# Turning q and k by 64 tokens on the two halves of TensorE's rows, and one PV and one weight turn for both tail steps, in a thresholded attention followed by a leaky-ReLU MLP

## The chip, the cores and the metric

The kernel runs on one core of a Trainium2 chip. Its time is the device time of one execution in microseconds (us); lower is better. The core has five engines that run side by side, each through its own list of instructions in order: TensorE (PE; its weight loads are shown as PEld), VectorE (DVE), ScalarE (ACT), GpSimd (POOL) and SyncE (SP), which issues most DMAs. TensorE writes to PSUM, eight banks per partition; GpSimd cannot read those, so VectorE and ScalarE empty them.

## What is computed

Eight batches of eight heads, 576 tokens, head dimension 64, in float32. Scores within `tau` of their row's maximum are kept, the others are dropped; the softmax of what is kept weighs `v`. The heads of a token are then joined to 512 features and go through a two-layer MLP with 2048 hidden features.

```python
    scale = 1.0 / np.sqrt(q.shape[-1])
    scores = scale * np.matmul(q, k.transpose(0, 1, 3, 2))
    thresh = np.max(scores, axis=-1, keepdims=True) - tau
    scores = np.where(scores >= thresh, scores, -1000000000.0)
    scores = scores - np.max(scores, axis=-1, keepdims=True)
    attn = np.exp(scores)
    attn = attn / (np.sum(attn, axis=-1, keepdims=True) + 1e-09)
    return np.matmul(attn, v).astype(np.float32)
...
    h = x @ w_in
    g = np.maximum(0.01 * h, h)
    return (g @ w_out).astype(np.float32)
```

## The kernel before

**Steps.** The work is a list of 144 steps, 18 per batch (`PERB`). A main step handles 128 query tokens of one pair of heads against all 576 keys: a batch has 2 blocks of 256 tokens x 4 pairs (`p`) x 2 halves (`c`), 16 steps. The last 64 tokens of a batch (512 to 575) are the tail: steps 16 and 17 of each batch take them, two pairs of heads at once. A loop over `n` (L487) writes out, for each `n`, instructions of several steps at different ages; every engine runs its instructions in just this order.

**q and k.** They arrive as float32 in `raw` tiles (`load_main`, 4 buffers) and `rawt` tiles for the tail (`load_tails`, 2 buffers). A unit is one pair of heads of q or of k, or the tail of q or k for all pairs: ten units per batch. GpSimd scales a unit by 64 and splits it into a high and a low fp16 half (`split_scale`, `split_high`, `split_low`, tile `half`). TensorE then turns it so that the head dimension lies on the partitions (`turn`, L162 to L188): 16 transposes for a main unit, 8 for a tail unit. Each has 64 columns of `half` over all 128 partitions as its weights and the 128 x 128 identity as the moving operand, and the two heads of a pair go to the upper and lower 64 output partitions, that is to the two halves of TensorE's columns. The result stands in one PSUM tile `tp` of the tag "h" and one VectorE copy moves a main unit, 128 x 1024 numbers, into `qT` or `kT`; a tail unit takes two copies of 128 x 256. L400 to L405 set when: the ten units of batch `b` from the third on are turned in steps 4, 5, 7, 9, 11, 13, 14, 16, 18 and 20 counted from the start of the batch before (`base`), with the GpSimd work three and two steps earlier. The units of batches 0 and 1 have times of their own.

**One pass of the loop.** Loads that are due (SP); `exps` of step n-1 (three ScalarE passes); `scores` of step n: 12 matmuls with 64 rows each, the two heads on the two halves of TensorE's rows, into the four PSUM banks of the tag "sc"; `copy_min` (VectorE: two passes out of PSUM that also give the row maxima); GpSimd's split work and `threshold` (GpSimd from step 28 on, VectorE before); `weights` of step n-1 (VectorE). Every second step, after a pair's second half, follow `recip` (VectorE), `widen` (GpSimd, writes the reciprocal beside the weights) and `turn_w`, a transposing DMA from SP that turns the weights `w` into `wT`. Then comes one unit of the first MLP layer (`layer1`, PSUM tile `hp` of the tag "h", emptied by ScalarE), the turns that are due, up to two pieces of the second layer (`layer2`, tag "o"), and `pv` with `evacuate`: the weighted sum of `v` for the step that is `PV_LAG` = 4 steps old, into the PSUM tag "pv", emptied by VectorE with a multiplication by the reciprocal.

**PSUM.** "sc" has four banks (one step's scores), "h" two, "pv" one and "o" one: all eight are taken.

**Tails.** Each tail step has its own pair tile, `recip`, `widen`, `turn_w` (128 x 1280), `pv` (20 matmuls of 64 columns) and `evacuate` (128 x 128). Tails of two batches make one group of 128 tokens for the MLP.

**The end.** After step 143 the loop runs on with what is left: the last PVs, `layer1` and `layer2` of the last groups, and the stores.

Of the kernel before, what the change touches and what calls it, by code (L numbers as in the profile page):

```python
# [10 lines left out]
FP16 = mybir.dt.float16  # L11
# [3 lines left out]
PV_LAG = 4  # L15
# [23 lines left out]
def kernel(  # L39
# [122 lines left out]
    def turn(key, copy=None):  # L162
# [24 lines left out]
        else:  # L187
            copy(out=dst[:, :, p, ds(c0, 512)], in_=tp[:, :, :, :].rearrange("d x t p -> d x (t p)"))  # L188

    steps = []
# [27 lines left out]
    def copy_min(st):  # L220

        st.mn = sb.tile([128, 2, 2], FP32, tag="mn", bufs=3, name="mn")
        st.s = sb.tile([128, 2, 576], FP32, tag="s", bufs=2, name="s")
        for h in range(2):
            nc.vector.tensor_scalar(  # L225
                out=st.s[:, h, :].rearrange("p (a b) -> p a b", a=2), in0=st.sc[h][:, :, 0:288],
                scalar1=-1.0 / UNIT, scalar2=None, op0=AX.mult, op1=AX.min, accum_out=st.mn[:, h, 0:1])

    def threshold(st):
        st.th = sb.tile([128, 2, 2], FP32, tag="th", bufs=3, name="th")  # L230
        eng = nc.vector if st.n < 28 else nc.gpsimd
        eng.tensor_scalar(out=st.th[:, :, 0], in0=st.mn[:, :, 0], scalar1=1.0, scalar2=tau_f, op0=AX.mult, op1=AX.add)  # L232

    def exps(st):

        c = 0 if st.tail else st.c
        if c == 0:
            pairs["now"] = pr = Pair()
            pr.w = sb.tile([128, 2, 10, 128], FP16, tag="w", bufs=3, name="w")
            pr.sum = sb.tile([128, 2, 2], FP32, tag="sum", bufs=3, name="sum")  # L240
            pr.n = 1 if st.tail else 2
        st.pair = pr = pairs["now"]
        flat = pr.w[:, c, :, :].rearrange("q n d -> q (n d)")
        st.w = [flat[:, ds(576 * h, 576)] for h in range(2)]
        st.sum = [pr.sum[:, c, h : h + 1] for h in range(2)]
        st.e = sb.tile([128, 576], FP16, tag="e", bufs=2, name="e")
        for h in range(2):
            if h:
                z = st.s[:, h, :]
                nc.scalar.activation(out=z, in_=z, func=AF.Prelu, bias=st.th[:, h, 0:1], scale=-1.0, alpha=1e20)  # L250
                nc.scalar.activation(out=st.w[h], in_=z, func=AF.Exp, bias=minus_tau[:, :], scale=1.0,  # L251
                                     accum_out=st.sum[h])
# [25 lines left out]
    def turn_w(pr):  # L278
        new_wt(pr)
        nc.sync.dma_start_transpose(out=pr.wt[:, 0 : pr.n, :, :].rearrange("k c n q -> k (c n) q"),  # L280
                                    in_=pr.w[:, 0 : pr.n, :, :].rearrange("q c n d -> q (c n d)"))
# [12 lines left out]
    def pv(st):  # L294
        st.pv = ps.tile([128, 4, 128], FP32, tag="pv", bufs=1, name="pv")
        wt = st.pair.wt
        for u in range(2 if st.tail else 1):
            for i in range(5):
                for h in range(2):
                    blk = i if h == 0 else 9 - i  # L300
                    rhs = wt[:, 0, blk - (blk > 4), ds(64 * u, 64)] if st.tail else wt[:, :, blk - (blk > 4), :]
                    o = st.pv[ds(64 * h, 64), 0, ds(64 * u, 64)] if st.tail else st.pv[ds(64 * h, 64), 0:2, :]
                    nc.tensor.matmul(out=o, lhsT=v16[st.b % 2][:, st.p + u, blk, :], rhs=rhs,  # L303
                                     start=(i == 0), stop=(i == 4), skip_group_check=True)

    groups = {}
# [1 line left out]
    def evacuate(st, n):  # L308
        wt = st.pair.wt
        if st.tail:  # L310
            if (st.b % 2, st.c) == (0, 0):
# [3 lines left out]
            nc.vector.tensor_tensor(  # L315
                out=xg.x[:, ds(st.p, 2), ds(64 * (st.b % 2), 64)],
                in0=st.pv[:, 0, :].rearrange("d (u q) -> d u q", u=2),
                in1=wt[:, 0, 9, :].rearrange("d (u q) -> d u q", u=2), op=AX.mult)
            done = (st.b % 2, st.c) == (1, 1)
        else:  # L320
            if st.p == 0:
                groups["m"] = xg = Group(256, (st.b, 2 * st.blk))
                xg.x = sb.tile([128, NP, 256], FP16, tag="x", bufs=3, name="x")
            xg = groups["m"]
            nc.vector.tensor_tensor(out=xg.x[:, st.p, :].rearrange("d (c q) -> d c q", c=2), in0=st.pv[:, 0:2, :],  # L325
                                    in1=wt[:, :, 9, :], op=AX.mult)
# [59 lines left out]
    def at(d, n, f):  # L386
        d.setdefault(n, []).append(f)

    def units(b):
        u = [(b, p, w_) for p in range(NP) for w_ in "kq"]  # L390
        return u[:2] + [(b, "t", "k")] + u[2:] + [(b, "t", "q")]

    for b in range(1, B):
        base = PERB * (b - 1)
        for i, (s, w_) in enumerate(((0, "k"), (0, "q"), (1, "k"), (1, "q"))):
            at(loads_at, base + ((-2, 0, 5, 7)[i] if b > 1 else (3, 4, 8, 9)[i]),
               lambda b=b, s=s, w_=w_: load_main(b, s, w_))
        for i, w_ in enumerate("kq"):
            at(loads_at, base + (2, 12)[i] + 4 * (b == 1), lambda b=b, w_=w_: load_tails(b, w_))
        for i, key in enumerate(units(b)):  # L400
            n_ = base + 4 + 18 * i // 10 if b > 1 else 9 + 3 * i // 2
            at(pool_at, n_ - 3, lambda key=key: split_scale(key))
            at(pool_at, n_ - 3, lambda key=key: split_high(key))
            at(pool_at, n_ - 2, lambda key=key: split_low(key))
            at(turns_at, n_, lambda key=key: turn(key, nc.vector.tensor_copy))  # L405
    for b in range(B):
        base = PERB * (b - 1)
        if b:
# [73 lines left out]
        at(turns_at, n_, lambda key=key: turn(key, nc.vector.tensor_copy if key[2] == "q" else None))  # L482

    N = len(steps)
    pv_at = {s.n + PV_LAG - s.early: s for s in steps if s.tail or s.c == 1}
    n = 0
    while n < N + PV_LAG + 2 or l1q or l2q or stores:  # L487
        for f in loads_at.get(n, []):
            f()
        if 1 <= n <= N:  # L490
            exps(steps[n - 1])
        if n < N:
            scores(steps[n])
            copy_min(steps[n])
        if n == 0:
            split_now(first[3])
            threshold(steps[0])
            split_now(first[4])
        if n == 1:
            turn(first[4], nc.vector.tensor_copy)  # L500
        if n < 11:
            idle(8 if n else 16)
        todo = pool_at.get(n, [])
        for f in todo[:1]:
            f()
        if 0 < n < N:
            threshold(steps[n])
        for f in todo[1:]:
            f()
        if 1 <= n <= N:  # L510
            last = steps[n - 1]
            weights(last)
            if last.early:
                recip(last.pair, last.c, 1)
                widen(last.pair, last.c, 1, nc.vector)
            elif last.tail or last.c == 1:
                recip(last.pair, 0, last.pair.n)
# [50 lines left out]
```

## Time and profile before

| | |
|---|---|
| time, median of 3 runs | 515.73 us (514.61 to 517.10) |
| the profiled execution: time, span | 515.1 us, 513.2 us |
| mean granted TensorE clock | 0.992 |
| VectorE, ScalarE, GpSimd busy, share of the span | 83%, 84%, 59% |
| DMA queue of SP, share of 16 engines | 77.5% |
| start of the scores of step 72, of step 143 | 249.3, 473.4 us |

The span runs from the first to the last instruction. A row of a group of instructions gives the line, the engine, the operation, what it writes and reads, partitions x elements and count, then busy time and mean duration of one, then idle time of the engine in front of them and what ended it. A row of the timeline gives start, length from the first start to the last end, engine, line and count; in brackets idle time of that engine before it. Matmuls are pipelined, so the spacing of their starts, not the duration of one, is what a matmul costs. A unit `64*128` on TensorE means that 64 rows and 128 columns of the array are used, `128*64` the other way round.

### The profile page before, as it was taken

To read this page: it belongs to the slowest core of one execution; us is meant where nothing else is said; L and a number is where in the kernel's file an instruction comes from. 1 tells how busy PE (TensorE), PEld (TensorE's weight loads), DVE (VectorE), ACT (ScalarE), POOL (GpSimd) and SP (SyncE) were. 2 spreads that over 40 slices of the span, in tenths; PEclk is the share of its full clock that TensorE was granted. 3 is DMA by queue.
4 is the path that set the end of the run, shared out by engine and by line. 5 is a ranking of instruction groups with operands and counts; after the bars stand their busy time and mean duration, and the time that the engine had idled before them with its cause. 6 is when DMAs were issued, how large, how long until landed. Compare 5 with 4: busy or idle time off the path is not lost.

```text
span 513.2 us, 19695 instructions
## 1 busy us (share of the span) xinstructions
PE 488.5 (95%) x8043; PEld 352.0 (69%) x8043; DVE 423.8 (83%) x1174; ACT 433.4 (84%) x781; POOL 305.3 (59%) x523
## 2 busy tenths in 40 slices
PE   7878798999999999999999999999999999999996
PEld 6656576657677777777676777777776777666884
DVE  4999999999898888888898888988898888888300
ACT  4977887789899989998899989998999989999532
POOL 4991578356776767666676767666776764223000
PEclk9989989999999999999999999999999999999999
DMA  8995787599989888878978999979988979666611
GB/s 246 237 204 98 146 183 151 129 190 168 239 166 183 201 188 192 173 149 210 206 178 177 203 187 192 168 156 212 183 203 159 202 166 158 135 117 138 144 43 63
DMA packets 220700, 87.79 MB, mean 171 GB/s; under 512 B 190913, under 2 KB 217537, under 8 KB 220609
## 3 DMA queue, kind: packets, MB, share of 16 engines
q1 hardware_dynamic: 217648, 82.07, 77.5%
q0 software_dynamic: 2688, 4.19, 4.7%
q8 instruction: 63, 1.03, 0.8%
q14 instruction: 29, 0.23, 0.1%
q10 hardware_dynamic: 272, 0.26, 0.1%
HBM read 36.70 MB, written 9.44 MB: 90 GB/s over the span
## 4 chain that ended last, share of the span: by engine, by line
PE 74%; DMA 4%; DVE 0%; ACT 0%; POOL 0%; issue 0%; DVEq 0%
PE hp L346 23%; PE o L362 18%; PE sc L217 18%; PE pv L303 6%; DMA wT<-w 4%; PE tp L177 4%; PE osc L362 3%; ACT osb L368 0%; DVE s L225 0%; DVE x L325 0%; POOL w L272 0%; DVE rec L269 0%; POOL half L148 0%; DVEq L325 0%; ACT s L250 0%
## 5 line engine op out<-in xcount | busy, mean ns | idle before, releaser
L225 DVE TENSOR_SCALAR_CACHE_REDUCE s<-sc 128x576 f32<-128x576 f32 x288 | 206.3, 753 | 33.6 <-PE sc L217 24.4
L346 PEld LDWEIGHTS <-win 128*64 128x64 f16 x2560 | 118.8, 110 | 35.0 <-issue 33.0
L217 PE MATMUL sc<-kT,qT 64*128 64x288 f16 (+1 forms) x1920 | 136.0, 286 | 5.3 <-DVE s L225 4.6
L346 PE MATMUL hp<-x,win 128*64 128x256 f16 x2048 | 137.6, 277 | 2.0 <-DVE x L325 2.0
L232 POOL TENSOR_SCALAR th<-mn 128x2 f32<-128x2 f32 x116 | 71.4, 616 | 113.1 <-ACT g L348 56.2
L362 PE MATMUL o<-wout,g 128*64 128x512 f16 x992 | 127.8, 379 | 0.0
L263 DVE SCALAR_TENSOR_TENSOR w<-s,th,e 128x576 f16<-128x576 f32 x144 | 126.3, 877 | 0.0
L251 ACT ACTIVATE w<-s,minus_tau 128x576 f16<-128x576 f32 x144 | 111.7, 776 | 9.4 <-DMA wT<-w 2.6
L217 PEld LDWEIGHTS <-qT 64*128 64x128 f16 (+1 forms) x1920 | 77.2, 97 | 57.2 <-issue 42.4
L250 ACT ACTIVATE s<-s,th 128x576 f32<-128x576 f32 x144 | 110.4, 767 | 4.1 <-POOL th L232 2.5
L254 ACT ACTIVATE e<-s,mn 128x576 f16<-128x576 f32 x144 | 110.2, 765 | 1.2 <-DVE s L225 1.2
L348 ACT ACTIVATE g<-hp 128x512 f16<-128x512 f32 x144 | 84.3, 586 | 28.6 <-PE hp L346 27.4
L362 PEld LDWEIGHTS <-g 128*64 128x64 f16 x1152 | 62.7, 110 | 29.7 <-issue 0.2
L148 POOL TENSOR_TENSOR half<-scaled,half 128x512 f16<-128x512 f32 (+1 forms) x75 | 79.9, 1065 | 1.7
L303 PE MATMUL pv<-wT,v 128*64 128x256 f16 (+1 forms) x960 | 54.1, 248 | 2.2 <-DMA wT<-w 2.2
L303 PEld LDWEIGHTS <-v 128*64 128x64 f16 x960 | 43.4, 111 | 18.0 <-issue 3.6
L177 PE MATMUL tp<-ident,half 128*64 128x128 f16 x1152 | 47.5, 223 | 4.3 <-DVE half L159 1.8
L272 POOL CAST w<-rec 128x256 f16<-128x256 f32 (+1 forms) x76 | 28.7, 378 | 38.3 <-DVE rec L269 35.1
L144 POOL CAST half<-scaled 128x512 f16<-128x512 f32 (+1 forms) x75 | 45.3, 604 | 7.6 <-PE tp L177 3.0
L177 PEld LDWEIGHTS <-half 128*64 128x64 f16 x1152 | 41.0, 112 | 6.7 <-issue 2.9
L138 POOL TENSOR_SCALAR scaled<-raw 128x512 f32<-128x512 f32 x60 | 38.0, 633 | 7.9 <-DMA raw<-in_k_dram 5.8
L325 DVE TENSOR_TENSOR x<-pv,wT 128x256 f16<-128x256 f32 x64 | 26.8, 419 | 7.0 <-PE pv L303 6.3
(44 smaller groups left out, 306.5 us busy)
## 6 DMA issues: line engine op xcount, KB each, us to landing
vraw<-in_v_dram SPq DMA_DIRECT2D x16, 512.0 KB, 4.7
out_dram<-osb SPq DMA_DIRECT2D x16, 512.0 KB, 4.5
raw<-in_k_dram SPq DMA_DIRECT2D x14, 512.0 KB, 4.4
raw<-in_q_dram SPq DMA_DIRECT2D x14, 512.0 KB, 4.7
win<-in_moe_w_in_dram POOLq DMA_DIRECT2D x4, 512.0 KB, 8.2
wout<-in_moe_w_out_dram POOLq DMA_DIRECT2D x4, 512.0 KB, 12.2
wT<-w SPq DMA_TRANSPOSE x76, 5.6
raw<-in_k_dram SPq DMA_DIRECT2D x4, 256.0 KB, 4.4
```

What stands on the lines that cost most here:

```text
L148: nc.gpsimd.tensor_tensor(out=halves[key][:, 1, 0:n, :, :], in0=scaled.pop(key)[:, 0:n, :, :], in1=halves[key][:, 0, 0:n, :, :], op=AX.sub ...
L177: nc.tensor.transpose(o, half[:, x, t, h, :], ident[:, :])
L217: nc.tensor.matmul(out=o, lhsT=lhs, rhs=turned[st.b, "k"][rows, kx, pair, ds(key0, 288)], start=(i == 0), stop=(i == 2), skip_group_check= ...
L225: nc.vector.tensor_scalar(out=st.s[:, h, :].rearrange("p (a b) -> p a b", a=2), in0=st.sc[h][:, :, 0:288], scalar1=-1.0 / UNIT, scalar2=No ...
L250: nc.scalar.activation(out=z, in_=z, func=AF.Prelu, bias=st.th[:, h, 0:1], scale=-1.0, alpha=1e20)
L251: nc.scalar.activation(out=st.w[h], in_=z, func=AF.Exp, bias=minus_tau[:, :], scale=1.0, accum_out=st.sum[h])
L254: nc.scalar.activation(out=st.e[:, :], in_=st.s[:, h, :], func=AF.Exp, bias=st.mn[:, h, 0:1], scale=-1.0)
L263: nc.vector.scalar_tensor_tensor(out=st.w[0], in0=st.s[:, 0, :], scalar=st.th[:, 0, 0:1], in1=st.e[:, :], op0=AX.is_le, op1=AX.mult, accum ...
L303: nc.tensor.matmul(out=o, lhsT=v16[st.b % 2][:, st.p + u, blk, :], rhs=rhs, start=(i == 0), stop=(i == 4), skip_group_check=True)
L346: nc.tensor.matmul(out=hp[ds(64 * u2, 64), jj, :], lhsT=w_in16[:, i, ds(128 * j + 64 * u2, 64)], rhs=g.x[:, i, :], start=(i == 0), stop=(i ...
L348: nc.scalar.activation(out=g.g[:, ds(nj * u, nj), :], in_=hp[:, :, :], func=AF.Prelu, bias=0.0, scale=1.0, alpha=0.01)
L362: nc.tensor.matmul(out=g.o[ds(64 * u2, 64), :], lhsT=g.g[:, j, ds(128 * m + 64 * u2, 64)], rhs=w_out16[:, j, :], start=(j == 0), stop=(j = ...
```

## The change

Two edits.

First, from the third batch on, a unit is turned by `turn_rows` instead of `turn`. One transpose takes 64 tokens (64 partitions of `half`, half `r`) of both heads as 64 x 128 weights, with the 64 x 64 block of the identity as the moving operand; the two halves `r` lie on the two halves of TensorE's rows and write two PSUM tiles, `tpr`[0] of the tag "pv" and `tpr`[1] of the tag "h". The transposes are placed directly behind the scores of the step, ahead of `layer1`. A unit keeps its number of transposes. Each half is emptied by VectorE copies of its own: for a main unit one of 128 x 512 per half, in runs of 64 with gaps of 64; `tpr`[1] right behind the threshold, `tpr`[0] behind `weights`, `recip`, `widen` and `turn_w`. The two tail units are turned together. The steps are 4, 6, 8 (both tails), 10, 12, 14, 16, 18 and 20 of the batch before, all even; GpSimd's work and the tails' loads (steps 1 and 3 in place of 2 and 12) move with them.

Second, the two tail steps of a batch share one pair tile: one `recip`, one `widen`, one `turn_w` (128 x 2560), one `pv` (40 matmuls) and one `evacuate` (128 x 256), all at the time of the second tail step.

```diff
+    def turn_rows(keys):
+        tp = [ps.tile([128, 2, 4, 64], FP16, tag=("pv", "h")[r], bufs=1 + r, name="tpr") for r in range(2)]
+        for i, key in enumerate(keys):
+            half = halves.pop(key)
+            for x in range(2):
+                for t in range(2 if key[1] == "t" else 4):
+                    for r in range(2):
+                        rows = ds(64 * r, 64)
+                        o = tp[r][:, i, 2 * x + t, :] if key[1] == "t" else tp[r][:, x, t, :]
+                        nc.tensor.transpose(o, half[rows, x, t, :, :].rearrange("p h d -> p (h d)"), ident[rows, rows])
+        def copy(r):
+            for i, (b, p, which) in enumerate(keys):
+                dst = turned_of(b, which)
+                if p == "t":
+                    c0 = MAIN if which == "q" else 0
+                    nc.vector.tensor_copy(out=dst[:, :, ds(2 * r, 2), ds(c0, 64)],
+                                          in_=tp[r][:, i, :, :].rearrange("d (x s) p -> d x s p", x=2))
+                else:
+                    c0 = 0 if which == "q" else 64
+                    nc.vector.tensor_copy(
+                        out=dst[:, :, p, ds(c0, 512)].rearrange("d x (t r p) -> d x t r p", t=4, r=2)[:, :, :, r, :],
+                        in_=tp[r][:, :, :, :])
+                if (p, which, r) == ("t", "k", 0):
+                    nc.gpsimd.tensor_copy(out=dst[:, :, :, 576:640], in_=dst[:, :, :, 0:64])
+        return copy
...
     def exps(st):
-        c = 0 if st.tail else st.c
+        c = st.c
...
-            pr.n = 1 if st.tail else 2
+            pr.n = 2
...
     def pv(st):
-        for u in range(2 if st.tail else 1):
+        for c, u in [(c, u) for c in range(2) for u in range(2)] if st.tail else [(0, 0)]:
...
+    ROWS = [(0, "k"), (0, "q"), ("t", "k"), ("t", "q")] + [(p, w_) for p in (1, 2, 3) for w_ in "kq"]
...
-            at(loads_at, base + (2, 12)[i] + 4 * (b == 1), lambda b=b, w_=w_: load_tails(b, w_))
-        for i, key in enumerate(units(b)):
-            n_ = base + 4 + 18 * i // 10 if b > 1 else 9 + 3 * i // 2
+            at(loads_at, base + (1, 3)[i] if b > 1 else (6, 16)[i], lambda b=b, w_=w_: load_tails(b, w_))
+        for i, key in enumerate(units(b) if b == 1 else ROWS):
+            n_ = 9 + 3 * i // 2 if b == 1 else base + (4, 6, 8, 8, 10, 12, 14, 16, 18, 20)[i]
+            key = (b,) + key[-2:]
...
-            at(turns_at, n_, lambda key=key: turn(key, nc.vector.tensor_copy))
+            if b == 1:
+                at(turns_at, n_, lambda key=key: turn(key, nc.vector.tensor_copy))
+            else:
+                at(rows_at, n_, key)
...
-    pv_at = {s.n + PV_LAG - s.early: s for s in steps if s.tail or s.c == 1}
+    pv_at = {s.n + PV_LAG - s.early: s for s in steps if s.c == 1}
...
             scores(steps[n])
+            turned_now = turn_rows(rows_at[n]) if n in rows_at else None
             copy_min(steps[n])
...
             threshold(steps[n])
+        if n in rows_at:
+            turned_now(1)
...
-            elif last.tail or last.c == 1:
+            elif last.c == 1:
                 recip(last.pair, 0, last.pair.n)
                 widen(last.pair, 0, last.pair.n)
                 turn_w(last.pair)
+        if n in rows_at:
+            turned_now(0)
```

`evacuate` writes the whole tail of a batch in one VectorE instruction accordingly, and closes the group after every second batch as before.

More of the change, by code (lines that the diff above doesn't have):

```diff
@@ L300, in pv @@
                     blk = i if h == 0 else 9 - i
-                    rhs = wt[:, 0, blk - (blk > 4), ds(64 * u, 64)] if st.tail else wt[:, :, blk - (blk > 4), :]
-                    o = st.pv[ds(64 * h, 64), 0, ds(64 * u, 64)] if st.tail else st.pv[ds(64 * h, 64), 0:2, :]
-                    nc.tensor.matmul(out=o, lhsT=v16[st.b % 2][:, st.p + u, blk, :], rhs=rhs,
+                    if st.tail:
+                        rhs = wt[:, c, blk - (blk > 4), ds(64 * u, 64)]
+                        o = st.pv[ds(64 * h, 64), c, ds(64 * u, 64)]
+                    else:
+                        rhs = wt[:, 0:2, blk - (blk > 4), :]
+                        o = st.pv[ds(64 * h, 64), 0:2, :]
+                    nc.tensor.matmul(out=o, lhsT=v16[st.b % 2][:, 2 * c + u if st.tail else st.p, blk, :], rhs=rhs,
                                      start=(i == 0), stop=(i == 4), skip_group_check=True)
@@ L310, in evacuate @@
         if st.tail:
-            if (st.b % 2, st.c) == (0, 0):
+            if st.b % 2 == 0:
                 groups["t"] = xg = Group(128, (st.b, None))
@@ L315, in evacuate @@
             nc.vector.tensor_tensor(
[L316 to L319, printed above, removed]
+                out=xg.x[:, :, ds(64 * (st.b % 2), 64)].rearrange("d (c u) q -> d c u q", c=2),
+                in0=st.pv[:, 0:2, :].rearrange("d c (u q) -> d c u q", u=2),
+                in1=wt[:, :, 9, :].rearrange("d c (u q) -> d c u q", u=2), op=AX.mult)
+            done = st.b % 2 == 1
         else:
@@ L391, in units @@
         return u[:2] + [(b, "t", "k")] + u[2:] + [(b, "t", "q")]
+    rows_at = {}
+    ROWS = [(0, "k"), (0, "q"), ("t", "k"), ("t", "q")] + [(p, w_) for p in (1, 2, 3) for w_ in "kq"]
     for b in range(1, B):
@@ L404 @@
             at(pool_at, n_ - 2, lambda key=key: split_low(key))
-            at(turns_at, n_, lambda key=key: turn(key, nc.vector.tensor_copy))
+            if b == 1:
+                at(turns_at, n_, lambda key=key: turn(key, nc.vector.tensor_copy))
+            else:
+                at(rows_at, n_, key)
     for b in range(B):
```

## Prediction

> **What bounds the kernel now.** I read the page first, then the windows by batch, then the waits.
>
> ```profile
> span 513.2 us, 19695 instructions
> PE 488.5 (95%) x8043; PEld 352.0 (69%) x8043; DVE 423.8 (83%) x1174; ACT 433.4 (84%) x781; POOL 305.3 (59%) x523
> ...
> 249.34:307.05 57.71, 57.71 (x1003) 41.11 (x1002) 50.82 (x140) 51.81 (x94) 39.87 (x69) 1.00 0.92 188
> 364.68:422.39 57.71, 57.71 (x1003) 41.11 (x1002) 50.92 (x141) 52.24 (x94) 40.30 (x70) 1.00 0.92 182
> ...
> 444.50:450.40 5.90, 5.90 (x84) 4.04 (x82) 4.97 (x14) 5.83 (x12) 1.65 (x3) 1.00 0.59 114
> ...
> PE sc L217 <- DVE s L225: 4.6, 11, 1.4
> PE pv L303 <- DMA wT<-w: 2.2, 5, 0.7
> PE hp L346 <- DVE x L325: 2.0, 3, 1.0
> ```
>
> TensorE is busy in every microsecond of the middle batches: a batch of 18 steps takes 57.7 us, VectorE works 50.9 of them and ScalarE 52. TensorE waits for others only for a few us in the whole run. So each us taken out of TensorE's list is a us of the time, until another engine or a wait comes in. The row at 444.50 says how far that goes: in the last batch nothing is turned, two steps take 5.90 us, TensorE is still full, and VectorE (4.97) and ScalarE (5.83) keep up. A pair of steps in the middle takes 57.71/9 = 6.41 us, so there is room down to 5.90.
>
> **What a turn costs on TensorE.** The timeline of two steps, then two narrow looks at weight loads, then a tail's PV.
>
> ```profile
> 251.08 0.61 PE L177 MATMUL tp<-ident,half 128*64 128x128 f16 x16
> ...
> 252.49 0.91 PE L217 MATMUL sc<-kT,qT 64*128 64x288 f16 x12
> 253.32 1.06 PE L346 MATMUL hp<-x,win 128*64 128x256 f16 x16
> ...
> 316.26 0.48 PE L303 MATMUL pv<-wT,v 128*64 128x64 f16 x20
> ...
> L177 PE MATMUL tp<-ident,half 128*64 128x128 f16 x1152 | 47.5, 223 | 4.3 <-DVE half L159 1.8 <-ACT g L348 1.0 <-DVE qT L188 0.8
> L303 PE MATMUL pv<-wT,v 128*64 128x64 f16 x320 | 7.8, 196 | 0.0
> ...
> 252.48 0.10 PEld L217 LDWEIGHTS <-qT 64*128 64x128 f16 x2 [0.41 <-issue]
> 252.48 0.11 PEld L217 LDWEIGHTS <-qT 64*128 64x128 f16 x4 [0.41 <-issue]
> ...
> 253.32 0.11 PEld L346 LDWEIGHTS <-win 128*64 128x64 f16 x2 [0.24 <-issue]
> 253.32 0.14 PEld L346 LDWEIGHTS <-win 128*64 128x64 f16 x4 [0.24 <-issue]
> ```
>
> Transposes run in pairs, one on each half of the array. Sixteen span 0.61 us from first start to last end; less one duration (0.22) and over the 7 spacings between 8 pairs that is 0.056 us a pair, 0.446 us a main unit. The new transpose moves 64 columns. The trace has such matmuls in the tail's PV: (0.48 - 0.196)/9 = 0.0316 us a pair, 0.253 us a unit. **Saved: 0.193 us a main unit, 0.096 a tail unit** (8 transposes).
>
> The weights of these PV matmuls have another shape (128 rows x 64 columns) than the new ones (64 x 128), so the price of the new pair has to be bounded. From below, half of today's 0.056 for half the columns is 0.028, which would be worth 54 x 8 x 0.0036 = 1.6 us more (54: 48 main units and 12 tail units counted half). From above, if one weight load of this shape could not be overlapped by the next, a pair would cost about the 0.10 us that one load lasts, and a unit 8 x 0.10 = 0.80. What speaks for the lower end is the narrow looks. Two loads of 64 x 128 end after 0.10 us and four after 0.11: a second pair of loads needs only some 0.01 to 0.02 us more. For 128 x 64 it is 0.11 and 0.14, so 0.03 more. A load of the new shape follows its predecessor sooner than the one whose rate of 0.0316 is measured. I take 0.0316.
>
> The Trainium skill has a rule against this. "TensorE: Matmul & The Clock Gate", section "LDWEIGHTS (loading the stationary operand)", says that a load takes its number of columns over 1.2 ns, whatever the rows: 107 ns for the new 128 columns, 53 for the old 64; an estimate by it is 0.85 us a unit, dearer than today. The same page's "Weight-path perf modes" makes an exception of loads with all 128 columns in 16 bits, which are read faster, and the narrow looks agree with the exception.
>
> Six batches (the third to the eighth) have 8 main and 2 tail units each: 6 x (8 x 0.193 + 2 x 0.096) = **-10.4 us**.
>
> **One switch more.** From the first scores to `hp` it is 253.32 - 252.49 = 0.83 us. The twelve scores have (0.91 - 0.285)/5 = 0.125 a pair, so the next pair would be due at 0.75; the 0.08 to 0.09 more is the change from halves of rows to halves of columns. The new turns stand on the scores' side of it, so the number of switches stays, but for one place: the turn at step 16 of a batch follows tail scores, which use quarters of the array. 6 x 0.09 = **+0.5 us**, and 0 to 1 as bounds.
>
> **VectorE's order around the new turns.** Here the first half of a turn waits for the "pv" bank, which `evacuate` of the step before must leave.
>
> ```profile
> 281.37 0.91 PE L217 MATMUL sc<-kT,qT 64*128 64x288 f16 x12
> 281.52 0.41 DVE L325 TENSOR_TENSOR x<-pv,wT 128x256 f16<-128x256 f32 x1
> 282.39 0.76 DVE L225 TENSOR_SCALAR_CACHE_REDUCE s<-sc 128x576 f32<-128x576 f32 x1 [0.46 <-issue]
> 283.76 0.81 DVE L263 SCALAR_TENSOR_TENSOR w<-s,th,e 128x576 f16<-128x576 f32 x1
> 284.09 0.91 PE L217 MATMUL sc<-kT,qT 64*128 64x288 f16 x12
> 284.68 0.18 DVE L269 RECIPROCAL rec<-sum 128x4 f32<-128x4 f32 x1
> 287.31 0.68 DVE L188 COPY qT<-tp 128x1024 f16<-128x1024 f16 x1
> 287.80 0.91 PE L217 MATMUL sc<-kT,qT 64*128 64x288 f16 x12
> 287.91 0.42 DVE L325 TENSOR_TENSOR x<-pv,wT 128x256 f16<-128x256 f32 x1
> 293.59 0.71 PE L303 MATMUL pv<-wT,v 128*64 128x256 f16 x10
> ...
> L180 DVE COPY qT<-tp 128x256 f16<-128x256 f16 x16 | 3.7, 271 | 0.0
> ...
> 109.11 0.91 PE L217 MATMUL sc<-kT,qT 64*128 64x288 f16 x12
> ...
> 109.94 0.41 DVE L325 TENSOR_TENSOR x<-pv,wT 128x256 f16<-128x256 f32 x1
> ...
> 320.08 0.28 DVE L315 TENSOR_TENSOR xt<-pv,wT 128x128 f16<-128x128 f32 x1
> ```
>
> The rows show an even step at 281.37, an odd one at 284.09 and the next even one at 287.80. `evacuate` ends 0.53 to 0.56 us after the even step's scores begin; the turn can begin at 0.75. **The wait is hidden by the scores, with 0.2 us to spare.** With two copies in place of one VectorE must still be on time. Two points, 256 numbers in 0.271 us and 1024 in 0.68, give 0.14 fixed and 0.53 ns a number: 512 cost 0.41 us, and as copies here overlap the next instruction by 0.08 (287.31 to 287.91 is 0.60), some 0.34 each. I take runs of 64 as no dearer, since the 256-number copy writes such runs already. The pair of steps on VectorE is then: four `copy_min` of 0.68, two `weights` of 0.75, `recip` with its gap 0.27, two copies of 0.34, `evacuate` 0.42, together 5.6 us. The pair on TensorE, of which one step had a turn, was 287.80 - 281.37 = 6.43 and becomes 6.43 - 0.193 = 6.24. So VectorE is ahead by 0.6 us a pair, and `evacuate` waits for PV, not for VectorE. Nothing to pay in the middle batches; from the other side, if `evacuate` came 0.2 us late behind that, each 0.1 more would cost 0.1 x 54 = 5 us.
>
> In two places VectorE is late. In the second batch it still computes the thresholds: at 109.94 `evacuate` begins 0.83 after the scores and ends at 1.24, 0.49 past the point. I take two such steps, **+0.9 us** (0 to 2). And behind the tail's PV `evacuate` ended at 320.36; it grows from 0.28 to about 0.42 and I put the loss at 0.1 in each of six batches, **+0.6 us** (0 to 1.2). What the merge frees (one `recip`, `widen` and the fixed part of an `evacuate` a batch) lies on engines with room: 0.
>
> **The weights' DMA.** The first copy stands ahead of `weights`, so `recip`, `widen` and `turn_w` come 0.34 us later in the step, while the PV that needs `wT` comes sooner.
>
> ```profile
> 285.67 3.06 SPq L280 DMA_TRANSPOSE wT<-w  x1
> ...
> DMA to landing us min/median/max: 3.6/5.9/7.8
> ...
> 240.83 7.80 DMA wT<-w
> ...
> rawt<-in_q_dram SPq DMA_DIRECT2D x16, 64.0 KB, 5.3
> ```
>
> (The second row is that of L280 between 140 and 420 us, the third from the chain of waits, the last from the DMA issues.) From `recip` (284.68) to its PV (293.59) are 8.91 us today. The PV stands 12.22 behind 281.37, and two turns in between shrink by 0.193 each, so 11.83 (the turns at steps 11 and 13 of the batch); `recip` moves from 3.31 to 3.65; 8.18 us are left. Today 0.99 of them pass from `recip` to the DMA's issue, so about 7.2 us are left for the landing. The median, 5.9, fits; the longest, 7.8, does not, and it makes TensorE wait already today (TensorE's 2.2 us of such waits above). One or two late ones a batch at some 0.2 to 0.3 make **+1.8 us**, with 0 below, as the 128 KB load of q tails moves away from step 12, where the longest lies, and 4 above. What is queued behind a waiting PV is everything on TensorE: the next scores and all after.
>
> **GpSimd and SP.** The splits move by a step or two at most and stay on steps of their own; GpSimd works 40 of 57.7 us. The q tails are loaded two steps ahead of their split (today four): 2 x 3.2 us against a landing of 5.3, hidden, and about 1 us a batch if not.
>
> **The end.**
>
> ```profile
> 477.81 2.89 SPq L280 DMA_TRANSPOSE wT<-w  x2
> 484.73 0.51 PE L303 MATMUL pv<-wT,v 128*64 128x64 f16 x20
> ```
>
> The last weight turn is issued at about 479.3 and now has twice the size; main ones take 4.9 to 5.9, so it lands at 484.2 to 485.2. Its PV, with the first tail's out of the way (0.51 less one duration: 0.31), stands at 484.4. **+0.2 us** (0 to 0.8).
>
> **Sum.** -10.4 + 0.5 + 0.9 + 0.6 + 1.8 + 0.2 = -6.4 us. The profiled execution took 515.1 us, 1.9 over its span, so 508.7; the median of the runs shown is 0.6 higher, so **509.3 us**. With the terms' bounds this case runs from 505 to 514.
>
> **Rivals.**
> *All of the gain.* No late `evacuate`, no late DMA: 515.7 - 10.4 + 0.5 = 505.8. For it: the q tails' load leaves the crowded steps, and TensorE stays full even at 5.90 us a pair. Against it: the second batch.
> *The copies eat the gain.* If strided copies out of PSUM or the thresholds made `evacuate` end 0.2 us past the point in each pair, 54 x 0.2 = 10.8 would cancel the 9.9: 516.6. Against it: 0.6 us of room a pair.
> *The weights' DMA decides (slower).* From `turn_w` to PV. It decides when landings lengthen by 1 us throughout, to a median of 6.9 against the 7.2 left: then about half the 54 pairs wait, at some 0.5 us, 13.5 us in place of 1.8, and the time is 509.3 + 11.7 = 521. A milder one, 0.6 us longer, a third of the pairs waiting 0.5, gives 9 in place of 1.8: 516.5. For it: the DMA engines have a share of 0.92 in the middle batches. Against it: at 0.59 (row of 444.50) the pairs also land and PV never waited there.
> *Weight loads do not overlap (slower).* At 0.80 a unit instead of 0.446 the turns cost 54 x 0.35 = 19 us more: 515.7 + 19 = 535. Against it the four loads in 0.11 us. At 0.056 a pair the turns would save nothing, and the losses of the sum, 4.0, would make 519.7. The skill's rule on columns would be this rival.
>
> **How the numbers follow.** The forecast 0.58, all of the gain 0.12, the copies 0.12, the DMA 0.12, the loads 0.06. Faster or slower counts from 0.5%, 2.6 us, about what runs of this kernel can tell from no change. Faster: the forecast but for its upper edge, and all of the gain, 0.68. Same: that edge, the copies and a part of the mild DMA case, 0.15. Slower: the rest, 0.17. The range goes from 504.5, under the full gain, to 518.5, which takes in the copies and the mild DMA case and leaves out the loads and the strong DMA case; the likeliest case alone is 505 to 514.
>
> **What would show it.** TensorE's transposes of 64 x 64 moved numbers spaced 0.03 us a pair, so `tpr` busy near 54 x 0.25 = 14 us for 864 of them; even steps of 2.95 us in the middle batches and a batch of 56 us in place of 57.7; TensorE's waits in front of `tpr` for `evacuate` below 2 us in sum, and in front of `pv` for `wT` near 3. It is wrong if the spacing is 0.05 or more, if TensorE waits for VectorE in front of `tpr` in most even steps, or if the wait for `wT` exceeds 8 us.

## The result, and the profile after

| | before | changed | ratio (95% interval) |
|---|---|---|---|
| time, median of 4 runs each | 516.12 us | 510.26 us | 0.9884 (0.9847 to 0.9922) |
| profiled execution: time, span | 515.1, 513.2 us | 509.6, 507.8 us | |

The change makes the kernel 5.9 us faster by the medians and 5.5 by the two profiled executions; 6.4 were forecast. The page of the changed kernel:

```profile
span 507.8 us, 19682 instructions
PE 477.4 (94%) x8043; PEld 343.7 (68%) x8043; DVE 417.0 (82%) x1206; ACT 432.1 (85%) x781; POOL 292.4 (58%) x515
```

Two of its new groups of instructions, the transposes and a copy:

```profile
L200 PE MATMUL tpr<-ident,half 64*128 64x64 f16 x864 | 21.5, 190 | 2.0 <-DVE xt L347 1.0 <-DVE x L357 0.9
L210 DVE COPY qT<-tpr 128x512 f16<-128x512 f16 x48 | 19.5, 407 | 0.0
```

Two of its waits (engine and line, awaited, us in total, times, longest):

```profile
PE sc L245 <- DVE s L253: 5.7, 15, 1.4
PE pv L335 <- DMA wT<-w: 5.0, 7, 1.1
```

Two numbers give the balance. TensorE is busy 477.4 us in place of 488.5: 11.1 less. It is idle 507.8 - 477.4 = 30.4 in place of 24.7: 5.7 more. The difference, 5.4, is the change of the span. So about half of what TensorE was relieved of is lost again to waits. The waits for `wT` grew by 2.8 us (2.2 before, 5.0 now), those of the scores for VectorE by 1.1 (4.6 before, 5.7 now), and 2.0 us in front of the new transposes are new; these three make nearly all of it.

The windows by batch, changed kernel, from the second batch to the seventh (us, then busy time of PE, PEld, DVE, ACT and POOL, granted clock, DMA share, GB/s):

```profile
74.70:134.54 59.84, 54.97 (x900) 38.01 (x900) 55.40 (x162) 50.78 (x92) 38.22 (x63) 1.00 0.86 179
134.54:190.23 55.69, 55.53 (x996) 39.78 (x996) 49.70 (x146) 51.62 (x95) 37.71 (x69) 1.00 0.87 191
190.23:247.35 57.12, 56.00 (x940) 39.99 (x940) 49.72 (x146) 53.53 (x98) 39.25 (x72) 1.00 0.97 189
247.35:303.25 55.90, 55.90 (x1004) 40.17 (x1004) 49.72 (x146) 50.25 (x93) 36.27 (x66) 1.00 0.87 192
303.25:360.01 56.76, 56.20 (x940) 39.93 (x940) 49.71 (x146) 53.03 (x97) 38.24 (x70) 1.00 0.93 183
360.01:417.24 57.23, 56.28 (x1004) 40.00 (x1004) 49.70 (x146) 51.81 (x96) 37.76 (x69) 1.00 0.96 189
```

The fifth batch (from 247.35) shows the change undisturbed: 55.90 us in place of 57.71, TensorE full. The fourth, sixth and seventh miss that by 0.9 to 1.3 us. By the starts of the scores most of it lies in one step, the last of the batch, which takes 4.57, 3.94 and 4.12 us in these three and 3.26 in the fifth. The second batch gains next to nothing: before, its window from 74.27 to 134.25 had 59.98 us.

The timeline of two steps of the changed kernel, TensorE first, then VectorE, and at the end the place at which `wT` was longest awaited:

```profile
259.76 0.91 PE L245 MATMUL sc<-kT,qT 64*128 64x288 f16 x12
260.51 0.40 PE L200 MATMUL tpr<-ident,half 64*128 64x64 f16 x16
260.83 1.06 PE L378 MATMUL hp<-x,win 128*64 128x256 f16 x16
262.69 0.91 PE L245 MATMUL sc<-kT,qT 64*128 64x288 f16 x12
263.53 1.06 PE L378 MATMUL hp<-x,win 128*64 128x256 f16 x16
...
262.14 0.42 DVE L210 COPY kT<-tpr 128x512 f16<-128x512 f16 x1
262.48 0.81 DVE L291 SCALAR_TENSOR_TENSOR w<-s,th,e 128x576 f16<-128x576 f32 x1
263.40 0.18 DVE L297 RECIPROCAL rec<-sum 128x4 f32<-128x4 f32 x1
266.05 0.42 DVE L357 TENSOR_TENSOR x<-pv,wT 128x256 f16<-128x256 f32 x1
...
237.77 0.61 SPq L93 DMA_DIRECT2D vraw<-in_v_dram  x1
238.53 4.40 SPq L308 DMA_TRANSPOSE wT<-w  x1
...
246.66 0.74 PE L335 MATMUL pv<-wT,v 128*64 128x256 f16 x10 [1.12 <-DMA wT<-w]
```

Sixteen new transposes span 0.40 us; less a duration of 0.19 and over 7 spacings that is 0.030 us a pair. The even step with a turn takes 262.69 - 259.76 = 2.93 us. Scores to `hp` is 1.07 us with a turn and 0.84 without: the turn costs 0.23. The PV at 246.66, in the last step of the fourth batch, waited 1.12 us for a weight turn issued at 238.53, which stands behind loads of `v` in SP's list.

### The profile page after: what moved, and what is told of

The parts are those of the page before. It is cut to its first block, busy times and chain, and to the rows that moved or that the text cites. A ratio compares the mean times of both kernels' runs of the same rounds, so it can differ in the third digit from the quotient of the medians.

```text
span 507.8 us, 19682 instructions
## 1 busy us (share of the span) xinstructions
PE 477.4 (94%) x8043; PEld 343.7 (68%) x8043; DVE 417.0 (82%) x1206; ACT 432.1 (85%) x781; POOL 292.4 (58%) x515
## 4 chain that ended last, share of the span: by engine, by line
PE 63%; DMA 9%; DVE 4%; issue 1%; ACT 1%; POOL 0%; DVEq 0%; POOLq 0%
PE hp L378 20%; PE sc L245 16%; PE o L394 16%; DMA wT<-w 9%; PE pv L335 6%; PE osc L394 3%; DVE s L253 2%; PE tpr L200 2%; DVE w L291 1%; DVE qT L210 0%; ACT s L278 0%; DVE rec L297 0%; DVE kT L210 0%; DVE x L357 0%; ACT w L279 0%
## 5 line engine op out<-in xcount | busy, mean ns | idle before, releaser
L291 DVE SCALAR_TENSOR_TENSOR w<-s,th,e 128x576 f16<-128x576 f32 x144 | 121.4, 843 | 0.0
L380 ACT ACTIVATE g<-hp 128x512 f16<-128x512 f32 x144 | 84.1, 584 | 31.1 <-PE hp L378 30.4
L260 POOL TENSOR_SCALAR th<-mn 128x2 f32<-128x2 f32 x116 | 51.9, 448 | 89.0 <-DVE s L253 59.0
L394 PEld LDWEIGHTS <-g 128*64 128x64 f16 x1152 | 65.4, 110 | 29.7 <-issue 0.2
L148 POOL TENSOR_TENSOR half<-scaled,half 128x512 f16<-128x512 f32 (+1 forms) x75 | 83.4, 1113 | 3.1
L300 POOL CAST w<-rec 128x256 f16<-128x256 f32 x68 | 27.0, 398 | 72.4 <-DVE rec L297 67.7
L335 PE MATMUL pv<-wT,v 128*64 128x256 f16 (+1 forms) x960 | 52.5, 247 | 5.1 <-DMA wT<-w 5.0
L335 PEld LDWEIGHTS <-v 128*64 128x64 f16 x960 | 41.0, 111 | 20.6 <-DMA wT<-w 6.7
L279 ACT ACTIVATION_READ_ACCUMULATOR w<-s,minus_tau 128x1 f32 x144 | 26.8, 186 | 0.0
L400 ACT ACTIVATE osb<-o 128x512 f32<-128x512 f32 x31 | 18.5, 597 | 8.3 <-PE o L394 8.3
```

Of the source, the lines that this page charges most:

```text
L148: nc.gpsimd.tensor_tensor(out=halves[key][:, 1, 0:n, :, :], in0=scaled.pop(key)[:, 0:n, :, :], in1=halves[key][:, 0, 0:n, :, :], op=AX.sub ...
L291: nc.vector.scalar_tensor_tensor(out=st.w[0], in0=st.s[:, 0, :], scalar=st.th[:, 0, 0:1], in1=st.e[:, :], op0=AX.is_le, op1=AX.mult, accum ...
L335: nc.tensor.matmul(out=o, lhsT=v16[st.b % 2][:, 2 * c + u if st.tail else st.p, blk, :], rhs=rhs, start=(i == 0), stop=(i == 4), skip_grou ...
L380: nc.scalar.activation(out=g.g[:, ds(nj * u, nj), :], in_=hp[:, :, :], func=AF.Prelu, bias=0.0, scale=1.0, alpha=0.01)
L394: nc.tensor.matmul(out=g.o[ds(64 * u2, 64), :], lhsT=g.g[:, j, ds(128 * m + 64 * u2, 64)], rhs=w_out16[:, j, :], start=(j == 0), stop=(j = ...
```

## Experiments

Each ratio is against runs of the kernel before that were taken together with the experiment; below 1 is faster than before. Versions that were not taken together are better compared by their ratios than by their times.

**1. The merge alone** (`merge_only`: kernel before, with the second edit alone). Core of the edit:

```diff
-    pv_at = {s.n + PV_LAG - s.early: s for s in steps if s.tail or s.c == 1}
+    pv_at = {s.n + PV_LAG - s.early: s for s in steps if s.c == 1}
...
-            pr.n = 1 if st.tail else 2
+            pr.n = 2
```

> Theory (the gain is the smaller moving operand of the new transposes): the merge of the tails alone is worth nothing on the path that sets the end, 515 to 517.5 us beside 516.1 of before. Rival (the merge carries part of the gain, by fewer instructions on VectorE and one long weight turn): 513 us or less.

Measured: 515.76 us, ratio 0.9998 (0.9983 to 1.0013). By itself the merge is worth nothing, as the theory said.

**2. The new turn alone** (`rows_only`: changed kernel with the second edit undone, the diff above the other way round).

> Theory: nearly all of the gain without the merge, 509 to 511.5 us; the waits of the turn for the tail's evacuate (0.996 us at 90.5 in the changed kernel) may go or move by some tenths. Rival (the merge carries part): 512.5 us or more.

Measured: 516.57 us, ratio 1.0013 (0.9998 to 1.0028). The theory falls: without the merge the new turn brings nothing, and yet the merge brings nothing without the turn. The timeline of step 2 of the fifth batch of `rows_only`, TensorE and VectorE:

```profile
255.13 0.91 PE L245 MATMUL sc<-kT,qT 64*128 64x288 f16 x12
255.88 0.40 PE L200 MATMUL tpr<-ident,half 64*128 64x64 f16 x16
257.10 1.03 PE L390 MATMUL o<-wout,g 128*64 128x512 f16 x8
259.31 0.51 PE L331 MATMUL pv<-wT,v 128*64 128x64 f16 x20 [1.18 <-DVE qT L210]
...
258.87 0.39 DVE L210 COPY qT<-tpr 128x512 f16<-128x512 f16 x1
```

and its group of PV matmuls:

```profile
L331 PE MATMUL pv<-wT,v 128*64 128x256 f16 (+1 forms) x960 | 53.8, 248 | 14.0 <-DVE qT L210 6.9 <-DMA wT<-w 6.4 <-DVE s L253 0.5
```

Separate tails put the first tail step's PV in an even step, the only one in a batch, and a turn (q of pair 3, step 20 of the batch before) stands in the same step. `tpr`[0] occupies the one "pv" bank until VectorE's second copy, which stands behind `weights` and `recip` and ends at 259.26. The PV waits 1.18 us for it, 6.9 us over the run.

**3. The same without that meeting** (`rows_only_3q`: as 2, with this one unit turned by the old `turn`, which uses the "h" banks).

```diff
-            if b == 1:
+            if b == 1 or key[1:] == (3, "q"):
                 at(turns_at, n_, lambda key=key: turn(key, nc.vector.tensor_copy))
```

> The new turn without the merge, but the last unit of a batch (q of pair 3, turned at step 20) by the old turn, so that no turn of the pv bank stands in the one even step that has a PV (that of the first tail step). New theory: rows without merge lost its gain there, a PV waiting 1.2 us a batch for the copy out of the pv bank, and step 2 of a batch goes back from 4.6 to about 3.5 us: 509.5 to 512.5 us. Rival (the separate tails cost by something else: their weight turns, VectorE, the two evacuates): 514 us or more.

Measured: 509.88 us, ratio 0.9877 (0.9855 to 0.9899), as fast as the changed kernel with the merge. The PV's waits for the turn, 6.9 us in `rows_only`, are gone. The waits for `wT` fall too, from 6.4 to 3.4 us; in that step no copy stands ahead of the weight turn any more, and the two effects were not separated. On the other side TensorE has 2.1 us more to do (480.4 us in place of 478.3). With that one turn out of the "pv" bank the merge makes no difference that these runs can tell: it pays by moving a PV out of the even steps, not by the work it saves.

**4. Old shape at the new place** (`cols_early`, `cols_early2`: old transposes right behind the scores, in the new steps, one copy per unit behind the weight turn).

```diff
-            turned_now = turn_rows(rows_at[n]) if n in rows_at else None
+            if n in rows_at:
+                turned_now = [turn(key, nc.vector.tensor_copy, later=True) for key in rows_at[n]]
...
-        if n in rows_at:
-            turned_now(1)
...
-            turned_now(0)
+            for f in turned_now:
+                f()
```

> The old transposes (weights of 128 x 64, 128 columns moved) at the new place and the new steps, one copy per unit behind the weight turn. Theory: the shape is the gain, 54 units x 0.2 us come back, 516 to 521 us. Rival (the gain is the place and the even steps, which level the steps): 510 to 512.5 us.

Measured: 535.5 us, ratio 1.0378 (1.0352 to 1.0405), far outside. Its timeline in step 8, where both tail units are turned:

```profile
287.94 1.92 PE L382 MATMUL hp<-x,win 128*64 128x256 f16 x16 [2.44 <-DVE kT L181]
```

Two units hold both "h" banks, and `hp` waits 2.44 us until their late copies; over the run these waits are 15.1 us. That is a fault of the experiment, not of the shape. `cols_early2` turns the q tails one step later:

```diff
-            n_ = 9 + 3 * i // 2 if b == 1 else base + (4, 6, 8, 8, 10, 12, 14, 16, 18, 20)[i]
+            n_ = 9 + 3 * i // 2 if b == 1 else base + (4, 6, 8, 9, 10, 12, 14, 16, 18, 20)[i]
```

> The old transposes at the new place as before, the q tails turned one step later than the k tails, so that no step holds both h banks. Theory (shape): even steps stay at 3.15 us against 2.93 of the changed kernel, step 8 falls from 5.8 to 7.4 us to about 3.2, and the time is 518 to 522 us less what the slower steps save in waits for the weights' DMA, some 2 us: 516 to 521 us. Rival (place and even steps are the gain): 510 to 512.5 us.

Measured: 514.53 us, ratio 0.9964 (0.995 to 0.9979). That is 1.5 us under the range of the theory and well above that of the rival. Its proper partner is `copies_last` (6 below), which has its copies in the same place and the new shape: 506.11 us, taken together with it. **The shape is worth 8.4 us**, with what hangs on it: two PSUM tiles, and two copies of half the size. An even step of `cols_early2` in the timeline:

```profile
254.26 0.91 PE L249 MATMUL sc<-kT,qT 64*128 64x288 f16 x12
255.10 0.64 PE L177 MATMUL tp<-ident,half 128*64 128x128 f16 x16
255.57 1.04 PE L382 MATMUL hp<-x,win 128*64 128x256 f16 x16
257.40 0.91 PE L249 MATMUL sc<-kT,qT 64*128 64x288 f16 x12
```

257.40 - 254.26 = 3.14 us against 2.93. The 0.21 us in each of 54 such steps would be 11.3; a part comes back, as TensorE waits 1.3 us for `wT` where `copies_last` waits 2.7, and 2.5 us in front of its new transposes besides. The 1.6 us by which this version beats the kernel before belong to place, steps and merge together; they were not taken apart, but none of it lies in the middle: by the starts of the scores its fifth batch takes 57.83 us, and 57.71 before.

**5. New shape at the old place** (`rows_late`: `turn_rows` and its copies behind `layer1`).

```diff
-            turned_now = turn_rows(rows_at[n]) if n in rows_at else None
...
             layer1()
+        if n in rows_at:
+            turned_now = turn_rows(rows_at[n])
+            turned_now(1)
+            turned_now(0)
```

> The new transposes, but behind the first MLP layer, where the array is split by columns. Theory: the transposes stay at 0.03 us a pair, but two changes between halves of rows and halves of columns are added for each turn, 0.09 to 0.13 us each, 53 steps: 10 to 14 us more than the changed kernel, 519 to 525 us. Rival (a change of the split costs nothing between short transposes, the place is of no account): 509 to 512 us.

Measured: 516.04 us, ratio 1.0003 (0.999 to 1.0017): no gain at all, though not the 519 to 525 that were expected. The start of an even step in its timeline:

```profile
294.89 0.91 PE L245 MATMUL sc<-kT,qT 64*128 64x288 f16 x12
295.73 1.06 PE L378 MATMUL hp<-x,win 128*64 128x256 f16 x16
296.72 0.41 PE L200 MATMUL tpr<-ident,half 64*128 64x64 f16 x16
```

and its group of PV matmuls:

```profile
L335 PE MATMUL pv<-wT,v 128*64 128x256 f16 (+1 forms) x960 | 52.8, 249 | 4.3 <-DMA wT<-w 3.7 <-DVE s L253 0.6
```

The transposes are as short as in the changed kernel (0.41 us for 16), and the even steps here, read off the starts of the scores in the trace, last 3.16 us, 0.23 more than 2.93. Two changes between halves of rows and halves of columns are added in them, 0.115 us each; 54 such steps make 12 us. The expectation added them to the time of the changed kernel. That was the wrong partner: here both copies of a turn stand behind the weight turn in VectorE's list, as in `copies_last` (6 below). Against its 506.11 us the place behind the scores is worth 9.9 us (10.2 by the ratios; the two were not taken together). Some 2 of the 12 us come back. TensorE waits 0.6 us in front of the new transposes, where `copies_last` waits 2.5, and the second batch is 1.1 us shorter (58.2 us between the starts of its scores and those of the third, in place of 59.3); the waits for `wT`, 3.7 us in place of 2.7, go the other way. How the rest divides I did not take apart.

**6. The wait for the weights' DMA**: three places of the copies, and a later PV.

```diff
-        if n in rows_at:
-            turned_now(1)
...
         if n in rows_at:
+            turned_now(1)
             turned_now(0)
```

is `copies_last` (both behind the weight turn); `copies_first` has both ahead of `weights`.

> The changed kernel with both copies of a turn behind the weight turn. Theory: recip and the weight turn are issued 0.34 us sooner, so the waits for the weights' DMA fall by 0.2 to 0.3 us in each of 7 places, 508 to 510 us. Rival (the copies now delay copy_min of the next step and so the scores): 511 us or more.

> The changed kernel with both copies of a turn ahead of weights, recip and the weight turn. Theory (each 0.34 us by which the weight turn is issued later costs waits for the weights' DMA; none ahead gave 506.1, one 510.3): two ahead give 512 to 516 us, with 8 us or more of TensorE's waits for wT. Rival (copies_last won because of VectorE's order alone, for instance the first copy waiting for the turn): 509 to 511 us, waits for wT near the 5.0 of the changed kernel.

The PV group of `copies_last`, with what its idle time waited for:

```profile
L335 PE MATMUL pv<-wT,v 128*64 128x256 f16 (+1 forms) x960 | 52.5, 247 | 2.7 <-DMA wT<-w 2.7
```

its group of new transposes:

```profile
L200 PE MATMUL tpr<-ident,half 64*128 64x64 f16 x864 | 21.5, 190 | 2.5 <-DVE x L357 1.5 <-DVE xt L347 1.0
```

and the PV group of `copies_first`:

```profile
L335 PE MATMUL pv<-wT,v 128*64 128x256 f16 (+1 forms) x960 | 52.6, 247 | 6.9 <-DMA wT<-w 6.9
```

| copies ahead of the weight turn | median | ratio (95% interval) | wait for `wT` |
|---|---|---|---|
| none (`copies_last`) | 506.11 us | 0.9806 (0.9784 to 0.9829) | 2.7 us |
| one (changed kernel) | 510.26 us | 0.9884 (0.9847 to 0.9922) | 5.0 us |
| two (`copies_first`) | 512.93 us | 0.9956 (0.9938 to 0.9973) | 6.9 us |

Each copy ahead costs: by the ratios 4.0 us for the first and 3.7 for the second. The waits for `wT` explain 2.3 and 1.9 of that; for the rest I can name no single place. `copies_last` did better than expected (508 to 510). The time of `copies_first` is in its range, but its waits are 6.9 us and not the 8 or more that were expected.

The other way to be early is to ask later: `lag6` takes the PV of steps 14 to 121 two steps later.

```diff
-    pv_at = {s.n + PV_LAG - s.early: s for s in steps if s.c == 1}
+    pv_at = {s.n + PV_LAG - s.early + (2 if 14 <= s.n < 122 else s.n in (122, 123)): s for s in steps if s.c == 1}
```

> The changed kernel with the PV of steps 14 to 121 two steps later. Theory (what is left of the gain is lost to late weight DMAs, 5.0 us of waits in 7 places): the waits from step 20 on, some 4 us, go, 506 to 508 us. Rival (the DMA engines themselves are short of time, so the wait moves to the next buffer or to ScalarE): 509 us or more.

Measured: 512.37 us, ratio 0.9926 (0.991 to 0.9942), 2.1 us slower than the changed kernel by the medians, though the intervals of the two ratios just overlap. The windows of `lag6`, from its fifth batch to its end:

```profile
245.58:301.50 55.92, 55.92 (x1002) 40.23 (x1000) 49.76 (x146) 52.40 (x96) 37.48 (x69) 1.00 0.90 192
301.50:357.32 55.82, 55.82 (x938) 40.15 (x936) 49.78 (x146) 51.47 (x94) 37.39 (x69) 1.00 0.97 191
...
413.40:466.13 52.73, 51.55 (x778) 35.71 (x776) 43.42 (x123) 48.15 (x88) 16.12 (x33) 1.00 0.74 135
466.13:510.45 44.32, 38.64 (x614) 28.00 (x612) 5.19 (x15) 18.38 (x32) 2.00 (x4) 0.99 0.29 76
```

and the last stretch of the changed kernel:

```profile
468.06:507.85 39.79, 35.10 (x566) 27.43 (x564) 5.03 (x15) 16.63 (x30) 1.94 (x4) 0.99 0.31 81
```

Neither theory nor rival: the middle batches lose their waits as the theory said (55.9 and 55.8 us, and the eighth batch begins at 413.40 in place of 417.24, 3.8 us ahead), and the DMA engines bear it at a share of 0.97. But by the starts of the scores the second batch, where the lag begins, takes 61.0 us in place of 59.84. In the eighth 1.9 us go where the lag goes back to 4 (a PV meets a turn's copy in an even step, as in 2), and the end takes 44.32 us in place of 39.79. TensorE has 3.5 us more to do there: `layer1` takes one unit a step, and two units more of it (32 matmuls), with 16 matmuls more of `layer2`, are left when the last scores begin.

**7. VectorE in the second batch** (`last_thr20`: `copies_last` with GpSimd computing the thresholds from step 20 on in place of 28).

```diff
-        eng = nc.vector if st.n < 28 else nc.gpsimd
+        eng = nc.vector if st.n < 20 else nc.gpsimd
```

> copies_last with the thresholds on GpSimd from step 20 on instead of 28. Theory (the second batch gains little because VectorE, which computes the thresholds there, brings evacuate late; TensorE waits some 3.5 us there): VectorE is relieved of 8 x 0.34 us, 504 to 505.5 us. Rival (GpSimd, which splits two batches' units there, is the slower place for them, or VectorE is late by the copies of the second batch's old turns): 506 us or more.

Measured: 504.88 us, ratio 0.9792 (0.977 to 0.9813), the fastest of all. The window of the second batch of `copies_last`:

```profile
74.40:133.70 59.30, 54.44 (x900) 37.70 (x899) 55.36 (x159) 49.83 (x90) 37.41 (x61) 1.00 0.86 178
```

the same of `last_thr20`:

```profile
74.30:132.50 58.20, 54.70 (x899) 37.95 (x900) 52.74 (x154) 50.49 (x92) 41.83 (x71) 1.00 0.89 182
```

and the group of its new transposes:

```profile
L200 PE MATMUL tpr<-ident,half 64*128 64x64 f16 x864 | 21.5, 190 | 0.1
```

VectorE works 2.6 us less in that batch, the batch is 1.1 us shorter, and the wait in front of the new transposes, 2.5 us in `copies_last`, is 0.1. The two ratios' intervals overlap, so by time alone the step from 506.1 to 504.9 is not settled; the place of the gain is as the theory said. TensorE is still idle for 3.5 us of that batch.

## Why the prediction was right, and where not

**The bound.** TensorE was full in the middle batches, so its savings were to come through; they did (fifth batch, 57.71 to 55.90). Right.

**The price of a turn.** 0.0316 us a pair were taken from the tail's PV; 0.030 were measured. In the step a turn costs 0.23 us, so a main unit saves 0.22 against its 0.446 of before, rather than 0.193. TensorE's busy time fell by 11.1 us where 10.4 - 0.5 were forecast. The rival of weight loads that do not overlap is out: sixteen transposes span 0.40 us, and by that rival a unit would take 0.80. One sign was put down wrongly: `tpr` is busy 21.5 us, not 14, because the 0.40 us of each of the 54 groups of sixteen include the duration of the last pair, which 54 x 0.25 left out. The Trainium skill's rule by columns ("TensorE: Matmul & The Clock Gate", section "LDWEIGHTS (loading the stationary operand)") would have given an estimate of 0.85 us a unit; nothing of that is seen. The times agree with the exception that the same page's "Weight-path perf modes" makes.

**One switch more.** 0.09 us were put at step 16 of a batch; the trace gives that step 3.06 us against 2.93, so 0.13. The Trainium skill, "TensorEngine Tiling (Array Packing)", section "Key Properties", says that a change of tiling mode drains TensorE. Experiment 5 agrees: two changes more cost 0.23 us, 0.115 each.

**VectorE and the pv bank.** In the middle batches nothing was to be paid, and nothing was: `evacuate` at 266.05 ends in time for the next turn, and all 2.0 us in front of `tpr` lie in the second batch. The 0.6 us for the tails' `evacuate` did not come in the middle batches, but one such wait stands in the second, here in the changed kernel's timeline with one for a main `evacuate`:

```profile
90.51 0.41 PE L200 MATMUL tpr<-ident,half 64*128 64x64 f16 x16 [1.00 <-DVE xt L347]
...
110.76 0.41 PE L200 MATMUL tpr<-ident,half 64*128 64x64 f16 x16 [0.76 <-DVE x L357]
```

That batch was to gain 1.7 (a sixth of 10.4) less 0.9 and gained 0.1, so its losses were put some 0.7 us too low. Experiment 7 shows VectorE's part: without the thresholds the same batch is 1.1 us shorter.

**The weights' DMA.** The mechanism was right: `recip` at 263.40 has its PV at 271.47, 8.07 us where 8.18 were worked out. The size was off: waits grew by 2.8 us, not 1.8.

```profile
DMA to landing us min/median/max: 4.8/6.5/8.1
```

This is the row of the weight turns between 140 and 420 us of the changed kernel (5.9 and 7.8 before). The median moved by 0.6 us too. That is the condition of the slower rival's milder form, but not its price: seven PVs waited, 5.0 us in sum, and not a third of 54. The merge alone does not move the median: it is 5.9 us in `merge_only`, where the short turns of single tails are gone as well. Nor does the median set the waits: in `copies_first` it is 6.2 us and the waits are longer, 6.9 us.

**The merge.** Here a step of the prediction was wrong, though the sum did not feel it. "What the merge frees lies on engines with room: 0" looked at the work saved. What counts is the place it empties: without it a PV and a turn meet in the one "pv" bank, and the whole gain is gone (experiments 2 and 3). That the forecast holds in this point is luck: the two edits came together. The queue behind a bank should have been listed step by step, as the queue behind a waiting instruction was. My expectation for experiment 2 repeated the mistake.

**The end.** 0.2 us were put there; from the last scores to the end it is 513.20 - 473.40 = 39.8 before and 39.79 after: 0.

**The sum.** 6.4 us were forecast and 5.9 measured. Part of that nearness is luck too: TensorE's list shrank by 1.2 us more than forecast, and its idle time grew by 5.7 us where 0.9 + 0.6 + 1.8 + 0.2 = 3.5 were put. The two errors have opposite signs.

## What to carry to other kernels

When two edits come together, price the meeting as well as each one: here one was worth nothing, the other was worth nothing alone, and both were worth 1.2%. A shorter instruction on the bounding engine must stand where the array's split does not change: the same transposes are worth about 10 us more behind the scores than behind the first layer, when the copies have the same place in both. A variant is to be compared with the one that differs from it in nothing else, which is not always the changed kernel. And what is put ahead of the start of a long transfer, even 0.34 us on an engine with room, costs once the transfer has little margin: moving the one copy that stood there behind it was a further 4 us, and `last_thr20` at 0.979 is faster than both kernels.

## What was not expected of the hardware

VectorE's busy time fell, 423.8 to 417.0 us, although it has 32 instructions more. The group of `weights` before:

```profile
L263 DVE SCALAR_TENSOR_TENSOR w<-s,th,e 128x576 f16<-128x576 f32 x144 | 126.3, 877 | 0.0
```

and after:

```profile
L291 DVE SCALAR_TENSOR_TENSOR w<-s,th,e 128x576 f16<-128x576 f32 x144 | 121.4, 843 | 0.0
```

That is 4.9 of the 6.8 us. Two rows of the timeline of before that lie side by side:

```profile
279.99 1.01 DVE L263 SCALAR_TENSOR_TENSOR w<-s,th,e 128x576 f16<-128x576 f32 x1
...
279.21 1.17 POOL L148 TENSOR_TENSOR half<-scaled,half 128x512 f16<-128x512 f32 x1
```

Of the 87 such instructions that begin between 140 and 420 us of the kernel before, 21 lasted 0.98 us or more, and in each of these cases GpSimd's subtraction of two tensors had begun earlier and still had 0.37 us or more to run. The others took 0.81 to 0.82 (283.76 in the prediction's rows). The excess follows what was left of the subtraction: 0.39 us left gave 1.00, 0.55 gave 1.16, and 1.11 gave 1.73, each time 0.81 plus what was left, less 0.2. In the changed kernel, whose splits stand at even steps, only one of them begins inside such a subtraction there, and it takes 0.89. Five meet a subtraction the other way round, VectorE first, as here:

```profile
268.66 0.81 DVE L291 SCALAR_TENSOR_TENSOR w<-s,th,e 128x576 f16<-128x576 f32 x1
...
267.28 0.67 POOL L148 TENSOR_TENSOR half<-scaled,half 128x256 f16<-128x256 f32 x1
268.84 1.16 POOL L148 TENSOR_TENSOR half<-scaled,half 128x256 f16<-128x256 f32 x1
```

VectorE keeps its 0.81, and GpSimd's subtraction takes 1.16 us where one of the same size, by itself at 267.28, takes 0.67. So in these rows the instruction that begins second takes longer. No run changed the meeting alone, so these rows are the whole evidence.
